# Sink-window attention and a SoLU layer on one core: value products of 15 chunks as 64x64 tiles, three more chunks' probabilities through DRAM, and a new order of all steps

## The chip, the cores and the metric

The kernel runs on one core of one Trainium2 chip. The metric is the time of one execution on the device in microseconds (us); of several runs the median is taken. Beside it there is one profiled execution, from which all rows below are read.

## The reference, cut to what matters

```python
def _attn_ref(q, k, v, n_sink, window):            # B=4, H=8, S=768, D=64; n_sink=4, window=128
    scores = matmul(q, k.T) / sqrt(D)
    rel = pos[:, None] - pos[None, :]
    keep = (pos[None, :] < n_sink) | ((rel >= 0) & (rel < window))
    a = softmax(where(keep, scores, -1e9))
    return matmul(a, v)

def _moe_ref(x, w_in, w_out, g_ln):                # x: [3072, 512] from the attention, d_ff=1024
    h = x @ w_in
    solu = h * softmax(h)
    ln = (solu - mean(solu)) / sqrt(var(solu) + 1e-6) * g_ln
    return ln @ w_out
```

All arrays are fp32. A query sees the four sinks and the 128 keys up to its own.

## The kernel before, in words

The 768 rows of each of the four batches are cut into 6 chunks of 128 rows, 24 chunks in all. They are numbered n in the order in which they are worked on: n = 0 and 1 are the first chunks of batches 0 and 1, 2 to 6 and 7 to 11 the other five of each, 12 to 17 batch 2 and 18 to 23 batch 3. `place(n)` gives (batch, chunk in the batch). Chunks 0, 1, 12 and 18 have no chunk before them; the other 20 see their own keys and those of the chunk before (`before(n)`).

A chunk goes through these steps: `turn_q`, `turn_k` (transposes), `score` (L659, L660: two products for each of 8 heads, into one of two PSUM banks), `pick` (DVE: each query takes of two key positions the one in its window, so that 128 columns hold the window), `mask` (DVE, with the row's maximum), `exps` (ScalarE), `invert` (DVE), `normalise` (GpSimd, for four heads at a time: a half-chunk, hb = 0 or 1), then the transpose of the probabilities, the masks, the value product, and the two layers. Each column of the picked probabilities belongs either to the own chunk or to the chunk before. After the transpose, `part_new` (L747) copies the part of the own chunk into `pc`, with zeros elsewhere, and `part_old` (L753) zeroes that part in `pt`.

The transpose is done in one of two ways. Either PE turns four heads (`turn_p`, L738) into PSUM and ScalarE copies them (`take_p`, L742), or, for the chunks that `carried` names, the probabilities are stored to DRAM (`store_p`), loaded in blocks of 32 (`load_p`, tile `pb`), and DVE flips the 32x32 blocks (`flip_p`, L731). The same two ways exist for the hidden activations u: `turn_u` on PE (L888), for the chunks that `direct` names, or `store_u`, `load_u` (tile `ub`) and `flip_u` (L878).

`value` (L801) makes for each pair of heads r and each head x of the pair two products, current and previous, into `acc` (tile `av`): x = 0 writes output partitions 0 to 63, x = 1 the other 64. Each fp32 product stands as two records in the trace. `value_sinks` (L790) puts the sinks' share into `acc` first. `x_hi` (ScalarE, L806) and `x_lo` (DVE, L810) split `acc` into two fp32r halves. `hidden` (L821, 24 products) makes h, `highest`, `solu_exp`, `solu` (L836), `centre`, `square` follow, and `project` (L908, 24 products of 512 columns) makes the output o, which `scale` and `store` write.

PSUM has two pages for transposes (pool `ps_tr`), two banks for scores, two for `acc`, o and the sinks' transposes (pool `ps_acc`), and two for h. The steps are listed by stage and chunk, and `ORDER`, a table of numbers, sets the order in which they are issued. Every engine and the DMA queue on SP run their instructions in that order, each with waits for what it reads and for the buffer that it writes. No scheduler moves them.

## Time and profile before

| | |
|---|---|
| time, median of 3 runs (lowest to highest) | 427.01 us (426.56 to 427.19) |
| profiled execution: time, span of its instructions | 427.17 us, 425.5 us |
| instructions | 8510 |
| TensorE, VectorE, ScalarE, GpSimd busy | 96%, 80%, 76%, 54% of the span |
| moved by DMA | 81.37 MB, 191 GB/s on average |

The span runs from the first to the last instruction; 1.7 us of the time lie outside it. Engines are PE (matmul), PEld (PE's weight loads, which run beside the matmuls), DVE, ACT (ScalarE), POOL (GpSimd), and SPq for SP's DMA queue. Busy time is the union of an engine's instructions; a matmul's end is modelled, so the distance between starts says more of PE than the durations.

### The profile page before, as it was taken

The page shows a single profiled execution, that of the slowest core. Times are in us where ns is not written, and L with a number is a line of the kernel's source. Part 1 is how long each engine was busy: PE and PEld are TensorE (multiplying, and loading weights), DVE is VectorE, ACT ScalarE, POOL GpSimd, SP SyncE. Part 2 cuts the span into 40 slices and gives each one's busy share as a digit, 9 for nine tenths or more (in the row PEclk, how much of TensorE's full clock was granted, in tenths as well). Part 3 has the DMA queues.
Part 4 walks back from the last instruction along what each step waited for, and adds up shares of the span by engine and source line. Part 5 has one row for each costly group of instructions (what it writes and reads, how often), then busy time and mean ns, then how long its engine had stood idle before and what let it go on. Part 6 is the DMA issues. An engine that isn't in the chain of part 4 may idle for free.

```text
span 425.5 us, 8510 instructions
## 1 busy us (share of the span) xinstructions
PE 409.9 (96%) x2507; PEld 334.0 (79%) x2507; DVE 338.7 (80%) x981; ACT 323.5 (76%) x865; POOL 231.8 (54%) x388
## 2 busy tenths in 40 slices
PE   4989999999999999999999999999999999999995
PEld 3546778788888878888888888888888888888885
DVE  2889999898898888898998887987898997673430
ACT  4899999999888876889798666868878866555451
POOL 6641547387776545588445855548455379136010
PEclk9999999999999999999999999999999999999999
DMA  8998479899899999999998999996757766822101
GB/s 236 353 302 186 114 185 150 151 160 185 205 195 222 214 214 241 224 253 235 195 207 219 238 227 224 220 249 170 208 149 212 217 171 190 233 66 102 48 26 55
DMA packets 164024, 81.37 MB, mean 191 GB/s; under 512 B 120188, under 2 KB 150788, under 8 KB 163972
## 3 DMA queue, kind: packets, MB, share of 16 engines
q1 hardware_dynamic: 163972, 80.77, 84.1%
q8 instruction: 22, 0.36, 0.4%
q14 instruction: 30, 0.25, 0.2%
HBM read 45.62 MB, written 23.72 MB: 163 GB/s over the span
## 4 chain that ended last, share of the span: by engine, by line
PE 81%; ACT 5%; DMA 5%; DVE 3%; issue 3%; SPq 2%; POOL 1%; DVEq 0%; POOLq 0%; ACTq 0%
PE o L908 28%; PE h L821 28%; PE av L801 8%; PE bank L659 5%; PE bank L660 4%; PE ptp L738 2%; DMA wraw<-in_moe_w_in_dram 2%; PE ws L446 1%; PE bank L657 1%; DMA kn<-in_k_dram 1%; DMA pb<-pd 1%; DVE qT L603 1%; PE av L790 1%; ACT wps L424 1%; DMA pd<-pn 1%
## 5 line engine op out<-in xcount | busy, mean ns | idle before, releaser
L688 ACT ACTIVATE sc<-sc,nmx 128x132 f32<-128x132 f32 (+1 forms) x192 | 75.8, 397 | 17.5 <-DVE nmx L677 16.7
L628 POOL TENSOR_TENSOR ring<-kf,ring 64x512 fp32r<-64x512 f32 x48 | 63.9, 1333 | 28.3 <-ACT ring L623 17.7
L908 PE MATMUL o<-w2h,uh 128*128 128x512 f32 (+1 forms) x200 | 78.9, 395 | 0.0
L821 PE MATMUL h<-w1h,xh 128*128 128x512 f32 x192 | 77.4, 403 | 0.8 <-DVE u L836 0.6
L908 PE MATMUL o<-w2l,uh 128*128 128x512 f32 (+1 forms) x200 | 77.2, 386 | 0.0
L908 PE MATMUL o<-w2h,ul 128*128 128x512 f32 (+1 forms) x200 | 76.8, 384 | 0.0
L821 PE MATMUL h<-w1h,xl 128*128 128x512 f32 x192 | 75.7, 394 | 0.0
L821 PE MATMUL h<-w1l,xh 128*128 128x512 f32 x192 | 75.4, 393 | 0.0
L677 DVE CUSTOM_DVE_ANT_0 sc<-bank,bias 128x132 f32<-128x132 f32 (+1 forms) x192 | 53.0, 288 | 7.5 <-PE bank L660 2.0
L659 PE MATMUL bank<-ring,qT 128*128 128x264 f32 (+1 forms) x176 | 51.6, 300 | 1.4 <-DVE qT L603 0.8
L710 POOL TENSOR_TENSOR pn<-sc,rs 128x512 f32<-128x512 f32 x26 | 28.4, 1091 | 40.4 <-DVE rs L697 39.2
L660 PE MATMUL bank<-ring,qX 128*128 128x264 f32 (+1 forms) x176 | 48.7, 283 | 0.0
L908 PEld LDWEIGHTS o<-w2h,ul 128*128 128x128 f32 x200 | 37.5, 188 | 8.1
L821 PEld LDWEIGHTS h<-w1h,xl 128*128 128x128 f32 x192 | 36.0, 188 | 9.7 <-DVE xl L810 1.6
L908 PEld LDWEIGHTS o<-w2h,uh 128*128 128x128 f32 x200 | 37.6, 188 | 6.8 <-issue 1.4
L706 POOL TENSOR_TENSOR sc<-sc,rs 128x528 f32<-128x528 f32 (+1 forms) x22 | 24.8, 1131 | 32.2 <-DVE rs L697 31.8
L659 PEld LDWEIGHTS bank<-ring,qT 128*128 128x128 f32 x176 | 33.1, 188 | 11.8 <-DVE nmx L677 4.2
L831 ACT ACTIVATE e<-h,nm 128x1024 f32<-128x1024 f32 x24 | 26.8, 1116 | 20.0 <-DVE nm L826 19.9
L821 PEld LDWEIGHTS h<-w1h,xh 128*128 128x128 f32 x192 | 36.1, 188 | 7.0 <-ACT xh L806 1.0
L908 PEld LDWEIGHTS o<-w2l,uh 128*128 128x128 f32 x200 | 37.7, 188 | 4.9
L747 POOL TENSOR_SCALAR_AFFINE_SELECT pc<-pt 128x512 f32<-128x512 f32 x40 | 26.7, 672 | 25.1 <-DVE pt L731 18.1
L821 PEld LDWEIGHTS h<-w1l,xh 128*128 128x128 f32 x192 | 36.2, 188 | 4.8
(146 smaller groups left out, 962.1 us busy)
## 6 DMA issues: line engine op xcount, KB each, us to landing
qX<-qT SPq DMA_DIRECT2D x88, 128.0 KB, 3.0
ud<-u SPq DMA_DIRECT2D x20, 512.0 KB, 3.8
ub<-ud SPq DMA_DIRECT2D x80, 128.0 KB, 3.2
pd<-pn SPq DMA_DIRECT2D x26, 256.0 KB, 3.0
pb<-pd SPq DMA_DIRECT2D x52, 128.0 KB, 3.8
vn<-in_v_dram SPq DMA_DIRECT2D x24, 256.0 KB, 4.6
out_dram<-ob SPq DMA_DIRECT2D x23, 256.0 KB, 2.8
kn<-in_k_dram SPq DMA_DIRECT2D x12, 384.0 KB, 5.7
```

The source lines that it names most:

```text
L628: nc.gpsimd.tensor_tensor(t[ROWS[1 - x]], src[ROWS[x]], t[ROWS[x]].bitcast(F32), op=ALU.subtract)
L659: nc.tensor.matmul(o, st["qT", n, x][:, r, :], rhs, start=True, stop=False)
L660: nc.tensor.matmul(o, st["qX", n, x][:, r, :], rhs, start=False, stop=True)
L677: nc.vector.tensor_tensor_reduce(out=st["sc", n, hb][:, j, c0:c1], in0=st["s", n, h].rearrange("p a x -> p (a x)")[:, c0:c1], in1=bias0 if ...
L688: nc.scalar.activation(sc[:, i, c0:c1], sc[:, i, c0:c1], AF.Exp, bias=nmx[:, i:i + 1], scale=-1.0, accum_out=ssum[:, i:i + 1])
L706: nc.gpsimd.tensor_tensor(sc[:, :, c0:c1], sc[:, :, c0:c1], rs.unsqueeze(2).to_broadcast([P, HB, c1 - c0]), op=ALU.mult)
L710: nc.gpsimd.tensor_tensor(pn.rearrange("p g h f -> p h g f"), sc[:, :, 4:SEG].rearrange("p h (g f) -> p h g f", f=32), rs.unsqueeze(2).uns ...
L747: nc.gpsimd.affine_select(pc, st["pt", n, hb], pattern=[[0, HB], [1, P]], compare_op=ALU.is_ge, fill=0.0, base=0, channel_multiplier=-1)
L801: nc.tensor.matmul(acc[ROWS[x], r, :], vals[:, 2 * r + x, :], p[:, 2 * jp + x, :], start=alone, stop=alone or (r, i) == (NPAIR - 1, 1))
L821: nc.tensor.matmul(st["h", n][:, cols], a[:, kt, :], w[:, kt, cols], start=(kt == 0 and m == 0), stop=(kt == KT1 - 1 and m == 2))
L831: nc.scalar.activation(e, st["h", n], AF.Exp, bias=st["nm", n], scale=1.0, accum_out=se)
L908: nc.tensor.matmul(st["o", n, i], a[:, kt % 4, :], part(w, kt)[:, i * wide:(i + 1) * wide], start=(kt == 0 and m == 0), stop=(kt == KT2 - ...
```

## The change

Chunks 7 to 11, 13 to 17 and 19 to 23 (15 chunks, `split`) form their values in another way. Of the picked probabilities of such a chunk, in the transposed tile the keys are rows and the queries columns. In each 64-row half of the keys one of the two products (own keys, keys of the chunk before) reaches into all 128 columns and the other into 64 only. Now `pt` stays whole but for its two diagonal 64x64 blocks, in which `part_old` keeps one side and `part_new` copies the other side into a `pc` of half the width. `value` makes for each r, x and 64-row half y a product of 128 columns with `pt` and one of 64 columns with `pc`. The halves y = 0 write `acc`, the halves y = 1 write a second page, "far". `take_far` (ScalarE) copies far to SBUF and `join` (DVE) adds it to `acc`, ahead of `x_hi` and `x_lo`. `acc` and far of these chunks lie in the two pages that the transposes use; o and the sinks' transposes have `ps_acc` without them.

Chunks 7, 12 and 18 now send their probabilities through DRAM as the others from 8 on did, and chunk 22 its u. All steps are numbered anew and `ORDER` is another permutation. The diff, cut to its core:

```diff
-FIRST_P, LAST_P = 8, 22
+FIRST_P, LAST_P = 7, 22
...
-    ps_tr = ctx.enter_context(tc.tile_pool(name="ps_tr", bufs=2, space=PSUM))
+    ps_tr = ctx.enter_context(tc.tile_pool(name="ps_tr", bufs=1, space=PSUM))
...
+    pages = [ps_tr.tile([P, 512], F32, name=f"page_{i}") for i in range(2)]
...
+    def split(n):
+        return n >= FIRST_P and place(n)[1] > 0
+
     def carried(n):
-        return FIRST_P <= n <= LAST_P and place(n)[1] > 0
+        return FIRST_P <= n <= LAST_P
...
+    HALVES = (slice(0, P // 2), slice(P // 2, P))
+
+    def keep(out, x, new):
+
+        lead = 1 if new else -1
+        nc.gpsimd.affine_select(out, x, pattern=[[0, HB], [lead, P // 2]], compare_op=ALU.is_ge,
+                                fill=0.0, base=-(lead < 0), channel_multiplier=-lead)
+
     def part_new(n, hb):
+        if split(n):
+            pc = st["pc", n, hb] = sb.tile([P, HB, P // 2], F32, tag="pc", name=f"pc_{n}_{hb}", bufs=3)
+            for y in range(2):
+                keep(pc[HALVES[y]], st["pt", n, hb][HALVES[y], :, HALVES[y]], y == 1)
+            return
...
     def part_old(n, hb):
+        if split(n):
+            for y in range(2):
+                t = st["pt", n, hb][HALVES[y], :, HALVES[y]]
+                keep(t, t, y == 0)
+            return
...
     def accumulator(n):
+        if ("acc", n) not in st and split(n):
+            st["acc", n] = page(("acc", n), 1)
+            st["far", n] = page(("far", n), 1)
...
+        if split(n):
+            old = st["vo", n] if ("vo", n) in st else st["vn", before(n)]
+            tiles = ((HALVES[0], acc, st["vn", n], old), (HALVES[1], st["far", n], old, st["vn", n]))
+            for r in range(NPAIR):
+                hb, jp = divmod(r, HB // 2)
+                for whole in (True, False):
+                    for y, (rows, to, *vals) in enumerate(tiles):
+                        for x in range(2):
+                            cols = slice(0, P) if whole else rows
+                            p = st["pt" if whole else "pc", n, hb]
+                            nc.tensor.matmul(to[ROWS[x], r, cols], vals[not whole][rows, 2 * r + x, :], p[rows, 2 * jp + x, :],
+                                             start=whole and y == 1, stop=not whole and (y == 1 or r == NPAIR - 1))
+            return
...
+    def take_far(n, _):
+        if split(n):
+            t = st["xf", n] = sb.tile([P, NPAIR, P], F32, tag="xl", name=f"xf_{n}", bufs=2)
+            nc.scalar.copy(t, st["far", n])
+            done("far", n)
+
+    def join(n, _):
+        if split(n):
+            acc = st["acc", n]
+            nc.vector.tensor_tensor(acc, acc, st["xf", n], op=ALU.add)
...
     def direct(n):
-        return n < 2 or n >= NCH - 2
+        return n < 2 or n == NCH - 1
...
-    2109, 3, 170, 1216, 2144, 1459, 1924, 1454, 1460, 302, 2140, 143, 147, 154, 156, 155, 203, 1491, 255, 2110, 1000,
+    150, 279, 311, 1355, 204, 4, 2195, 159, 316, 2157, 740, 206, 254, 1520, 2190, 1482, 1517, 2156, 172, 1489, 314,
```

What the change makes of the instructions is seen at two places. The first is PE at chunk 8's values. Before, eight rows, each a pair of products x = 0 and 1, stand as follows (`pc` own part, `pt` previous part; `vn_8` and `vn_7` the values of the two chunks; the last row is an output product of chunk 5):

```order
L801 MATMUL av_8_2137<-pc_8_0_2169,vn_8_1947 64x128 x2
L801 MATMUL av_8_2137<-pt_8_0_2139,vn_7_1407 64x128 x2
L801 MATMUL av_8_2137<-pc_8_0_2169,vn_8_1947 64x128 x2
L801 MATMUL av_8_2137<-pt_8_0_2139,vn_7_1407 64x128 x2
L801 MATMUL av_8_2137<-pc_8_1_2171,vn_8_1947 64x128 x2
L801 MATMUL av_8_2137<-pt_8_1_2152,vn_7_1407 64x128 x2
L801 MATMUL av_8_2137<-pc_8_1_2171,vn_8_1947 64x128 x2
L801 MATMUL av_8_2137<-pt_8_1_2152,vn_7_1407 64x128 x2
L659 MATMUL bank_1_90<-ring_127,qT_10_0_1983 128x264
```

Now there are sixteen such rows, of which these are the first eight (`page_0` is acc, `page_1` is far):

```order
L840 MATMUL page_0_91<-pt_8_0_2151,vn_8_1935 64x128 x2
L840 MATMUL page_1_92<-pt_8_0_2151,vn_7_1490 64x128 x2
L840 MATMUL page_0_91<-pc_8_0_2181,vn_7_1490 64x64 x2
L840 MATMUL page_1_92<-pc_8_0_2181,vn_8_1935 64x64 x2
L840 MATMUL page_0_91<-pt_8_0_2151,vn_8_1935 64x128 x2
L840 MATMUL page_1_92<-pt_8_0_2151,vn_7_1490 64x128 x2
L840 MATMUL page_0_91<-pc_8_0_2181,vn_7_1490 64x64 x2
L840 MATMUL page_1_92<-pc_8_0_2181,vn_8_1935 64x64 x2
```

Rows of 128 columns alternate with rows of 64, and each goes to the two pages in turn. After the block PE has one score and nine products of o_5 before the first product of h_8 in the order before, and nine products of o_5 alone in the new one.

The second place is DVE between those two blocks, chunk 8's values and chunk 8's hidden product. Before (u_7 is the solu of chunk 7, 1024 columns):

```order
L697 RECIPROCAL rs_9_1_2145<-rs_9_1_2145 128x4
L836 SCALAR_TENSOR_TENSOR u_7_2220,nmu_7_2221<-h_7_2005,e_7_2149 128x1024
L603 TENSOR_TENSOR qT_10_1_2214<-qf_10_1907,qT_10_1_2214 64x512
L810 TENSOR_TENSOR xl_8_2230<-av_8_2137,xh_8_2218 128x512
L603 TENSOR_TENSOR qT_11_0_2210<-qf_11_1729,qT_11_0_2210 64x512
```

And now:

```order
L705 RECIPROCAL rs_9_1_2155<-rs_9_1_2155 128x4
L685 ISA sc_10_0_2163,nmx_10_0_2164<-bank_1_90,bias2_116 128x132
L685 ISA nmx_10_0_2164 128x1
L861 TENSOR_TENSOR page_0_91<-page_0_91,xf_8_2255 128x512
L897 SCALAR_TENSOR_TENSOR u_7_2260,nmu_7_2261<-h_7_2041,e_7_2252 128x1024
L869 TENSOR_TENSOR xl_8_2275<-page_0_91,xh_8_2258 128x512
L611 TENSOR_TENSOR qT_11_1_2157<-qf_11_1553,qT_11_1_2157 64x512
```

The join (L861) has come in ahead of u_7, and x_lo (L869) follows u_7; a rest_q that stood between them is elsewhere.

## Rows read from the trace of the kernel before

**Rows 1.** The page's first part (busy us, share of the span, instructions) and lines of the second (the span in 40 slices, busy share in tenths; PEclk is the granted clock in tenths of full speed).
```profile
PE 409.9 (96%) x2507; PEld 334.0 (79%) x2507; DVE 338.7 (80%) x981; ACT 323.5 (76%) x865; POOL 231.8 (54%) x388
PE   4989999999999999999999999999999999999995
PEclk9999999999999999999999999999999999999999
```
**Rows 2.** Busy time by stretch: the stretch, its length, then busy us and instructions of each engine, granted clock, DMA share, GB/s.
```profile
0.00:120.00 120.00, 109.52 (x645) 84.51 (x646) 100.72 (x301) 106.78 (x281) 70.76 (x116) 1.00 0.96 204
120.00:360.00 240.00, 239.60 (x1491) 198.95 (x1490) 210.03 (x625) 186.37 (x520) 145.44 (x239) 1.00 0.94 212
200.00:220.00 20.00, 20.00 (x136) 16.65 (x135) 18.90 (x57) 17.74 (x51) 8.34 (x14) 1.00 1.15 208
```
**Rows 3.** The longest waits of PE (what waited, for whom: us in total, times, longest), and from the view of the tile av the line on who waited for its instructions.
```profile
PE bank L564 <- DMA kn<-in_k_dram: 4.2, 1, 4.2
PE bank L657 <- ACT val L311: 1.2, 1, 1.2
...
  PEld h L821: 2.6, 7
```
**Rows 4.** The chain that ended last: its shares by engine (from the page), and pieces of it (start us, us, what).
```profile
PE 81%; ACT 5%; DMA 5%; DVE 3%; issue 3%; SPq 2%; POOL 1%; DVEq 0%; POOLq 0%; ACTq 0%
...
151.34 4.23 DMA pb<-pd
...
158.55 1.90 PE av L801 x32
...
160.89 2.08 PE o L908 x9
```
**Rows 5.** PE's transposes: four in a row in the timeline (start us, us, engine, line, operation), and the two groups by line (count | busy us, mean ns).
```profile
207.13 0.60 PE L738 MATMUL ptp<-ident,sc 128*128 128x128 f32 x4
...
L738 PE MATMUL ptp<-ident,sc 128*128 128x128 f32 x88 | 13.2, 274 | 0.1
L888 PE MATMUL utp<-ident,ud 128*128 128x128 f32 x32 | 5.3, 274 | 0.0
```
**Rows 6.** Timeline of PE in a value block (chunk 11).
```profile
204.18 0.44 PE L801 MATMUL av<-pc,vn 128*64 128x128 f32 x4
204.44 0.39 PE L801 MATMUL av<-pt,vn 128*64 128x128 f32 x4
204.66 0.39 PE L801 MATMUL av<-pc,vn 128*64 128x128 f32 x4
```
**Rows 7.** Timeline of the first scores of chunk 1, products of 64 rows: heads 0 and 1 at 24.76 us, head 2 alone at 25.75 us; weight loads and products.
```profile
24.76 0.30 PEld L657 LDWEIGHTS bank<-kf,qf 64*128 64x128 f32 x4 [0.56 <-ACT qf L591]
24.76 0.49 PE L657 MATMUL bank<-kf,qf 64*128 64x128 f32 x4
...
25.75 0.29 PEld L657 LDWEIGHTS bank<-kf,qf 64*128 64x128 f32 x2 [0.69 <-DVE nmx L677]
25.75 0.48 PE L657 MATMUL bank<-kf,qf 64*128 64x128 f32 x2 [0.49 <-DVE nmx L677]
```
**Rows 8.** Weight loads of 64 and of 128 columns: from the view of L801 (durations in ns, min/median/max), and a group by line.
```profile
L801 PEld LDWEIGHTS av<-pt,vn x368: 132/137/137, 35.3 to 392.7; 128*64 128x64 f32 x184
...
L908 PEld LDWEIGHTS o<-w2h,ul 128*128 128x128 f32 x200 | 37.5, 188 | 8.1
```
**Rows 9.** DVE groups by line (count | busy us, mean ns | idle before, released by), three instructions in a row in the timeline, and DVE's longest wait.
```profile
L731 DVE STREAM_TRANSPOSE pt<-pb 128x512 f32<-128x512 f32 x26 | 17.4, 690 | 2.1 <-DMA pb<-pd 2.0
L810 DVE TENSOR_TENSOR xl<-av,xh 128x512 fp32r<-128x512 f32 x24 | 16.4, 683 | 2.7 <-ACT xh L806 2.6
L836 DVE SCALAR_TENSOR_TENSOR u<-h,e 128x1024 f32<-128x1024 f32 x24 | 29.2, 1218 | 4.4 <-ACT e L831 4.1
...
188.65 1.26 DVE L731 STREAM_TRANSPOSE pt<-pb 128x512 f32<-128x512 f32 x2
189.83 0.67 DVE L569 STREAM_TRANSPOSE kf<-kn 128x512 f32<-128x512 f32 x1
...
DVE bank L666 <- PE bank L660: 14.6, 27, 1.2
```
**Rows 10.** A ScalarE group by line: copies of a 128x512 tile out of PSUM.
```profile
L806 ACT CAST xh<-av 128x512 fp32r<-128x512 f32 x24 | 14.0, 583 | 5.5 <-PE av L801 5.4
```
**Rows 11.** GpSimd groups by line: the masks, a smaller one of the same kind, and GpSimd's longest wait.
```profile
L747 POOL TENSOR_SCALAR_AFFINE_SELECT pc<-pt 128x512 f32<-128x512 f32 x40 | 26.7, 672 | 25.1 <-DVE pt L731 18.1 <-ACT pt L742 6.7
L753 POOL TENSOR_SCALAR_AFFINE_SELECT pt<-pt 128x512 f32<-128x512 f32 x40 | 25.7, 654 | 1.6
L318 POOL TENSOR_SCALAR_AFFINE_SELECT scratch_f<-scratch_f 128x128 f32<-128x128 f32 x2 | 0.6, 299 | 0.1
...
POOL pn L710 <- DVE rs L697: 39.2, 13, 7.0
```
**Rows 12.** DMA issues from the page (count, KB each, median us from issue to landing).
```profile
ud<-u SPq DMA_DIRECT2D x20, 512.0 KB, 3.8
ub<-ud SPq DMA_DIRECT2D x80, 128.0 KB, 3.2
pd<-pn SPq DMA_DIRECT2D x26, 256.0 KB, 3.0
pb<-pd SPq DMA_DIRECT2D x52, 128.0 KB, 3.8
```

More of the change, by code (lines that the diff above doesn't have):

```diff
@@ L247, in _banded, with claim @@
     banks = [ps_s.tile([P, 512], F32, name=f"bank_{i}") for i in range(2)]
+    pages = [ps_tr.tile([P, 512], F32, name=f"page_{i}") for i in range(2)]
     held = {}
-    def claim(key, uses):
-        held[key] = [banks.pop(0), uses]
+    def claim(key, uses, free=banks):
+        held[key] = [free.pop(0), uses, free]
         return held[key][0]
@@ L256, in done, with page @@
         if held[key][1] == 0:
-            banks.append(held.pop(key)[0])
+            t, _, free = held.pop(key)
+            free.append(t)
+    def page(key, uses):
+        return claim(key, uses, pages).rearrange("p (j x) -> p j x", x=P)
     ident = cpool.tile([P, P], F32, name="ident")
@@ L735, in turn_p @@
         sc = st["sc", n, hb]
-        tr = st["ptp", n, hb] = ps_tr.tile([P, HB, P], F32, tag="tr", name=f"ptp_{n}_{hb}")
+        tr = st["ptp", n, hb] = page(("ptp", n, hb), 1)
         for j in range(HB):
@@ L810, in x_lo @@
         nc.vector.tensor_tensor(xl, st["acc", n], st["xh", n].bitcast(F32), op=ALU.subtract)
+        if split(n):
+            done("acc", n)
     NH = DFF // 512
@@ L884, in turn_u @@
         if ("utp", n, g4) not in st:
-            st["utp", n, g4] = ps_tr.tile([P, 4, P], F32, tag="tr", name=f"utp_{n}_{g4}")
+            st["utp", n, g4] = page(("utp", n, g4), 2)
         for j in (2 * r, 2 * r + 1):
@@ L892, in u_hi @@
         nc.scalar.copy(uh, st["utp", n, g4])
+        if direct(n):
+            done("utp", n, g4)
     def u_lo(n, g4):
@@ L937, in _banded @@
         take_p: kept(NHB), store_p: carries(NHB), load_p: carries(4), flip_p: carries(NHB), part_new: NHB, part_old: NHB, sinks_hi: NHB, sinks_lo: NHB, sink_values: 1, turn_sinks: 1,
-        take_sinks: 1, value_sinks: 1, value: 1, x_hi: 1, x_lo: 1, hidden: KT1 * NH, highest: 1,
+        take_sinks: 1, value_sinks: 1, value: 1, take_far: 1, join: 1, x_hi: 1, x_lo: 1, hidden: KT1 * NH, highest: 1,
         solu_exp: 1, solu: 1, floor_of: 1, centre: 1, square: 1, root: 1, store_u: flips(1), load_u: flips(4), flip_u: flips(KT2 // 4),
```

5 lines of the change are left out of this document (added), and 271 rows, old and new, of the table ORDER.

## The prediction, made before the changed kernel was run

> **What bounds the kernel now.** I read the shares of the engines first [rows 1]: TensorE (PE) is busy 96% of the 425.5 us span, VectorE (DVE) 80%, ScalarE 76%, GpSimd 54%. A busy PE need not be a full one, so the stretches come next [rows 2]: from 120 to 360 us PE is busy 239.60 of 240 us, and the waits of PE [rows 3] sum to a few microseconds, most of them at the start, on the first keys and on the weights. The chain that ended last [rows 4] says the same: 81% of it is PE, where a step follows the step before it on PE. So between about 80 us and the end the time is the sum of what PE issues, and the question is how much shorter that sum gets and whether the other engines can follow. DVE is the one to watch: 210.03 us busy in those 240 us, 87.5%, and at most 18.90 of 20 us (94.5%) in a stretch where PE was still full [rows 2].
>
> The profiled execution took 427.17 us with its 1.7 us around the span; the median of the runs shown is 427.01. I sum from 427.2.
>
> **The value product on PE.** Before, a chunk that has a chunk before it makes 16 products (two halves of heads x, four pairs r, current and previous values), each 128 rows deep, 64 output partitions, 128 columns. The trace has two records for each such product: 32 records in 1.90 us, drain into the next instruction included [rows 4]. One fp32 record of 128 columns alone takes 0.11 us from start to start: four transposes of this size take 0.60 us, of which the last one's own 0.27 us [rows 5]. In the value block four records start every 0.22 us [rows 6]. So two run at a time: the products x=0 and x=1 stand in different column halves of the array, and a step of 0.109 us serves both. 32 records are 16 steps, 1.74 us.
>
> After, each product is cut into two 64-row halves as well (y), of which one is whole (128 columns) and one is a 64-column part: 64 records, as four independent 64x64 tiles. The halves y write different PSUM pages (the accumulator and "far"). Do row halves run together too? The value block of before cannot show it, but another line does: for chunk 1 the scores are 64-row products (128 columns, fp32, two records each), and heads 0 and 1 stand in different row halves. At 24.76 us both were free to go: four records took 0.49 us; at 25.75 us one head alone, two records, took 0.48 us [rows 7]. Two row halves therefore cost what one costs. With rows and columns both split, I take four records for one step. A step of whole records is 0.109 us as before. A step of 64-column parts lies between half of that, 0.055 us, and 0.109 us (nothing won by fewer columns). What could hold it up is the weight load: 64 columns take 137 ns against 188 ns for 128 [rows 8], so 51 ns for 64 columns beside the fixed part, and in the old block such loads hide under the products. I take 0.057 us. The block is then 8 x 0.109 + 8 x 0.057 = 1.33 us, 0.41 us less than 1.74. Entering and leaving the tiled mode happens once per chunk before and after. 15 chunks: **-6.2 us** (bounds of the part step: 0 to -6.5 us).
>
> **Transposes that leave PE.** Chunks 7, 12 and 18 no longer turn their probabilities on PE (8 transposes each) and chunk 22 no longer turns its u (8): 32 x 0.109 = **-3.5 us** [rows 5]. PE's sum falls by 9.7 us.
>
> **What it adds elsewhere.** DVE: 15 joins (accumulator + far, 128x512 out of PSUM), 6 more flips of probabilities, 2 of u. Such instructions last 0.68 to 0.69 us, but follow each other every 0.6 us: two flips take 1.18 us up to the next start [rows 9]: 23 x 0.6 = 13.8 us. ScalarE: 15 copies of "far" more, 6 copies of turned probabilities less, at the 0.58 us of x_hi's copies from PSUM [rows 10]: +5.2 us, on an engine with a fifth of its span idle. GpSimd: a half-chunk's two masks of 128x512 (0.67 and 0.65 us) become four of 64x256. A 128x128 one takes 0.30 us [rows 11]; between the two, 0.42 us is my estimate, so 1.68 for 1.33 us, +10.6 us over 30 half-chunks. GpSimd then stands near 58%, and its idle time, most of it waits for DVE's reciprocals (the same group), covers this. DMA: four chunks more go out to DRAM and back (landing in 3.0 and 3.8 us for probabilities, 3.8 and 3.2 us for u [rows 12]), 23 more issues on SP's queue and some 4 MB more on 81; they are issued chunks ahead, and I count them at nothing. If one comes late, the price is what the chain once paid for such a load, 4.2 us [rows 4].
>
> **The longer chain behind a value block.** Before, x_hi (ScalarE, 0.58 us) and x_lo (DVE, 0.68 us) stood between the block and the hidden product; now the copy of "far" and the join come ahead of them: 2.5 us instead of 1.3. PE has other work there. The shortest covers in the new order are 9 output products behind chunk 8 (9 x 0.231 = 2.08 us, as the chain's x9 piece shows [rows 4]) and about as much behind chunk 13; behind chunk 8 stands the worse case, with the solu of chunk 7 (1.22 us [rows 9], 1.15 to the next start by my estimate) between join and x_lo on DVE. x_lo is needed only by the third hidden product, so 2.08 + 0.46 us stand against 0.58 + 0.6 + 1.15 + 0.68 = 3.0: about 0.5 us lost there, little or nothing behind the others. Before, PE lost 2.6 us in all on x_lo and x_hi [rows 3].
>
> **DVE as the next bound.** From 120 to 360 us, 12 joins and 6 flips add 10.8 us to 210.0: 220.8. PE needs 240 - 12 x 0.41 - 24 x 0.109 = 232.5 us for the same work, so DVE would stand at 95.0%. The densest row with PE full is 94.5% [rows 2], the mean 87.5%. At 94.5% the stretch takes 233.7 (+1.2 us), at 87.5% 252.3 (+19.8 us). I stay near the dense end, since DVE's longest wait is the one for PE's scores, 14.6 us [rows 9], which come sooner when PE is quicker: 94%, 234.9 us, +2.4 us, and with the lost half microsecond behind chunk 8 **+3 us**.
>
> Sum: 427.2 - 6.2 - 3.5 + 3.0 = **420.5 us**. Its own range is 417.5 (no stall at all) to 425.
>
> This is where the Trainium skill speaks against the change. "TensorEngine Tiling (Array Packing)", Performance Considerations, says that tiling speeds up the products but not the emptying of PSUM, which can become the bottleneck; here the tiling even adds a PSUM copy and a PSUM add per chunk. The rows of DVE above bear the rule out as a danger, and the first rival is what it would do.
>
> **Rivals.**
> A. *DVE becomes the bound.* Break-even is where the stretch takes 232.5 + 9.7 = 242.2 us, a DVE share of 91.2%. At 90% the stretch takes 245.3 and the kernel 430.3 us. For it: 18 more instructions in the stretch on an in-order engine, and the mean share. Against: the 20 us row with 18.90 and a full PE. Chance 0.12, on both sides of no change.
> B. *Row halves do not run together in 64x64 tiles.* The block is 16 x 0.109 + 16 x 0.057 = 2.66 us, +0.92 us: 427.2 + 13.7 - 3.5 = 437.4 us. Decided by one thing, the step for four records; it turns slower above 1.97 us a block. Against it stand the two heads in 0.49 us; for it only that no row shows four tiles. Chance 0.08. This is the rival on the other side.
> C. *PE cannot start records fast enough.* The new block needs one every 21 ns on average, the old one had one every 54 ns, and no row shows a denser run. If 54 ns were a limit, 64 x 0.054 = 3.5 us and the kernel some 450 us. "TensorE: Matmul & The Clock Gate", Part 1, gives a floor of about 25 ns from start to start however few columns; by it the block is 1.6 us and the kernel near 424.6 us. Up to 28 ns a record the kernel still gains a little (64 x 0.028 = 1.79 us a block, less the transposes, plus the 3 us). What speaks against a limit near 54 ns: the four weight loads of two heads took 0.30 us together, the two of one head 0.29 [rows 7], so twice the records came in the same time. Chance 0.10, half of it faster than before.
> D. *Better than the sum.* The first 120 us hold 10.5 us in which PE is not busy [rows 2]; all steps are re-ordered, and 3 us of that could go: 414.5 us. Chance 0.08. I see no difference in what the early weights need, so the re-ordering counts for nothing in the forecast.
>
> **How the numbers follow.** Forecast 0.62, D 0.08, A 0.12, C 0.10, B 0.08. A change within 0.2% (0.85 us) is about what a measurement of this kernel cannot tell from none. Faster by more: 0.62 + 0.08 + 0.03 of A + 0.05 of C = 0.78; within: 0.03 of A + 0.02 of C = 0.05; slower: 0.06 + 0.03 + 0.08 = 0.17. Leaving out B, the slow end of C and the far end of D gives 415 to 430.
>
> **What would show it.** Value block: 64 records, about 1.3 us of steps, 0.41 us less; whole-record steps of 0.11, part steps of 0.055 to 0.06. If blocks last 2.6 us, B; 1.6 us or more with even spacing, C. PE busy from 120 us on stays above 98%, and DVE at 94% or more of it; PE waits that name the join, x_hi or x_lo beyond 5 us in all, or scores waiting for masks on DVE, mean A. Transposes: 64 for probabilities and 24 for u. The prediction is wrong if PE's sum does not fall by some 9 us, or if it falls and new idle time on PE is more than about 6 us.

## The result: 1.1% slower, where 1.5% faster was forecast

The changed kernel takes **431.33 us** (median of 4 runs, 430.23 to 434.28); the kernel before, beside it, 426.84 us (426.56 to 427.19). The ratio is 1.0113, 95% interval 1.0091 to 1.0136: slower, and outside the range of 415 to 430. The profiled execution of the changed kernel took 430.23 us, its span is 428.5.

The rows that answer [rows 1] are from the first three parts of its page. PE is busy 94% instead of 96%, VectorE (DVE) 82%, GpSimd (POOL) the 58% forecast. The line DMA gives the busy share of the 16 DMA engines in tenths, the last row the program's own DMA traffic (packets, MB, share of the span).

```profile
PE 404.9 (94%) x2955; PEld 325.9 (76%) x2955; DVE 352.7 (82%) x1004; ACT 327.2 (76%) x874; POOL 248.4 (58%) x450
PE   4899999999999898999998999999999999999995
DMA  8999199999899998996999999995998878523311
...
q1 hardware_dynamic: 169588, 84.96, 87.0%
```

By stretch, as in [rows 2] (stretch, length, busy us of PE, its weight loads, DVE, ScalarE, POOL, granted clock, DMA share, GB/s):

```profile
0.00:120.00 120.00, 108.19 (x644) 82.80 (x645) 102.29 (x303) 106.55 (x281) 72.12 (x117) 1.00 0.97 204
140.00:160.00 20.00, 17.55 (x140) 13.93 (x140) 15.74 (x49) 14.36 (x43) 8.58 (x19) 1.00 1.15 212
220.00:240.00 20.00, 18.50 (x101) 15.03 (x101) 17.79 (x58) 16.87 (x51) 6.71 (x11) 1.00 1.19 220
80.00:300.00 220.00, 212.70 (x1614) 173.84 (x1613) 195.62 (x571) 173.78 (x480) 143.72 (x249) 1.00 1.05 216
120.00:360.00 240.00, 232.52 (x1827) 189.64 (x1826) 214.84 (x628) 186.35 (x518) 153.73 (x279) 1.00 0.98 224
```

From 120 to 360 us PE is busy 232.52 of 240 us; before it was 239.60. In none of the rows is another compute engine full: DVE has 15.74 of 20 us where PE misses most. The DMA engines are the only full ones, and they were full before as well, with PE full beside them. The same stretch from 80 to 300 us in the kernel before:

```profile
80.00:300.00 220.00, 219.60 (x1374) 183.10 (x1374) 192.48 (x568) 176.06 (x491) 138.47 (x219) 1.00 1.05 214
```

**Work and lost time.** I gave each record of PE the usual distance to the next start for its kind (0.231 us for 512 columns, 0.12 for 264, a value block its undisturbed length) and call what is over lost. Work falls from 391.6 to 382.0 us: values 42.1 to 36.1, transposes of probabilities 9.9 to 7.2, of u 3.7 to 2.7. That is 9.6 us, and 9.7 was forecast. Lost time grows from 31.3 to 44.2 us: from 24.1 to 25.1 before 120 us, from 4.1 to 15.7 between 120 and 280, from 3.1 to 3.5 behind. 427.2 - 9.6 + 12.9 = 430.5 us is the profiled time to 0.3 us. So the question is the 12.9.

The longest waits of PE answer [rows 3] (in all, times, longest); the first of them was not there before, the second and the fourth belong to the start:

```profile
PE bank L668 <- DMA qX<-qT: 5.1, 6, 1.7
PE bank L572 <- POOL mine L383: 4.1, 1, 4.1
PE bank L665 <- DVE nmx L685: 1.5, 4, 0.8
PE spread L312 <- DVE alone L306: 1.3, 1, 1.3
```

qX is q with its two halves swapped by DMA, for the second product of each score. The chain that ended last, whose shares answer [rows 4], has less of PE and more of DMA and all others:

```profile
PE 60%; DMA 10%; ACT 8%; DVE 7%; POOL 5%; issue 5%; SPq 4%; DVEq 0%; POOLq 0%; ACTq 0%
```

A chain followed back through one such place, from 134 to 144 us (start us, us, what):

```profile
134.73 4.37 DMA pb<-pd
...
139.23 0.72 DVE pt L744
...
140.01 0.43 POOL pc L763
...
140.98 0.42 POOL pt L763
...
141.88 0.26 SPq L733
...
142.23 0.59 SPq L620
```

This is chunk 7, whose probabilities now come through DRAM. Its load lands 4.4 us after its last issue, DVE has stood still 1.1 us for it, four masks follow (the first of each kind is shown), for the end of which SP's queue stands 0.3 us at a store (L733) before it issues the next swap of q (L620). The swap ahead of it is the one for which PE waited 1.67 us at 142.8. Its issue held SP's queue from 135.74 to 139.38 (timeline of SP):

```profile
135.74 3.64 SPq L620 DMA_DIRECT2D qX<-qT  x1
```

The four loads of chunk 7 stand ahead of that issue, from 132.69 to 135.17. The wait in it the profile puts down to ScalarE's `uh` (the waits of SP from 134 to 144 us), which itself had waited for a load of u to be flipped:

```profile
SPq L620 <- ACT uh L953: 2.5, 1, 2.5
```

The waits between scores are the larger loss, some 7 us more than before. The second new loss, 4.3 us, lies inside value blocks. A block in which nothing waits is as forecast: here the last part of one and its way out (records of one group overlap):

```profile
211.80 0.40 PE L840 MATMUL page<-pt,vn 64*64 64x128 f32 x8
212.02 0.29 PE L840 MATMUL page<-pc,vn 64*64 64x64 f32 x8
212.13 0.40 PE L840 MATMUL page<-pt,vn 64*64 64x128 f32 x8
212.35 0.29 PE L840 MATMUL page<-pc,vn 64*64 64x64 f32 x8
212.58 0.50 PE L973 MATMUL o<-w2h,uh 128*128 128x512 f32 x1
```

Eight records of 128 and eight of 64 columns take 0.33 us, two steps of 0.109 and two of 0.057. The block takes 1.35 us from the first to the last start and 0.15 out of it (1.70 and 0.20 before). But eight of the fifteen blocks took 1.40 to 2.67 us, waiting for the masks. In the longest, from 161.95 us, PE waits for these (timeline of POOL, start us, us):

```profile
160.12 0.91 POOL L763 TENSOR_SCALAR_AFFINE_SELECT pc<-pt 64x256 f32<-64x256 f32 x2 [7.22 <-DVE pt L744]
161.09 0.89 POOL L763 TENSOR_SCALAR_AFFINE_SELECT pt<-pt 64x256 f32<-64x256 f32 x2
162.05 0.89 POOL L763 TENSOR_SCALAR_AFFINE_SELECT pc<-pt 64x256 f32<-64x256 f32 x2
163.00 0.89 POOL L763 TENSOR_SCALAR_AFFINE_SELECT pt<-pt 64x256 f32<-64x256 f32 x2
```

GpSimd idled 7.22 us ahead of them: it is not short of time, its work comes late, and the masks then take 3.8 us in a row. Against [rows 12], the medians from issue to landing went from 3.0 to 3.9 us (stores of probabilities), 3.0 to 3.3 (swaps), 3.8 to 4.1 (stores of u), and 3.8 to 3.4 for the loads of probabilities:

```profile
qX<-qT SPq DMA_DIRECT2D x88, 128.0 KB, 3.3
ud<-u SPq DMA_DIRECT2D x21, 512.0 KB, 4.1
...
pd<-pn SPq DMA_DIRECT2D x32, 256.0 KB, 3.9
pb<-pd SPq DMA_DIRECT2D x64, 128.0 KB, 3.4
```

### The profile page after: what moved, and what is told of

The parts are those of the page before. It is cut to its first block, busy times and chain, and to the rows that moved or that the text cites. A ratio compares the mean times of both kernels' runs of the same rounds, so it can differ in the third digit from the quotient of the medians.

```text
span 428.5 us, 9560 instructions
## 1 busy us (share of the span) xinstructions
PE 404.9 (94%) x2955; PEld 325.9 (76%) x2955; DVE 352.7 (82%) x1004; ACT 327.2 (76%) x874; POOL 248.4 (58%) x450
## 4 chain that ended last, share of the span: by engine, by line
PE 60%; DMA 10%; ACT 8%; DVE 7%; POOL 5%; issue 5%; SPq 4%; DVEq 0%; POOLq 0%; ACTq 0%
PE o L973 21%; PE h L882 20%; DMA pb<-pd 4%; PE bank L667 4%; PE page L840 3%; PE bank L668 3%; DMA qX<-qT 3%; PE av L849 2%; DMA ub<-ud 2%; POOL pt L763 2%; ACT sc L696 2%; DVE qT L611 2%; DVE sc L685 1%; PE ws L454 1%; DMA qn<-in_q_dram 1%
## 5 line engine op out<-in xcount | busy, mean ns | idle before, releaser
L636 POOL TENSOR_TENSOR ring<-kf,ring 64x512 fp32r<-64x512 f32 x48 | 64.4, 1342 | 20.7 <-ACT ring L631 16.6
L721 POOL TENSOR_TENSOR pn<-sc,rs 128x512 f32<-128x512 f32 x32 | 34.1, 1066 | 38.4 <-DVE rs L705 23.9
L882 PEld LDWEIGHTS h<-w1h,xl 128*128 128x128 f32 x192 | 36.0, 188 | 10.5 <-DVE xl L869 2.6
L668 PEld LDWEIGHTS bank<-ring,qX 128*128 128x128 f32 x176 | 33.1, 188 | 11.0 <-DMA qX<-qT 6.5
L882 PEld LDWEIGHTS h<-w1h,xh 128*128 128x128 f32 x192 | 36.1, 188 | 7.1 <-ACT pt L755 0.9
L763 POOL TENSOR_SCALAR_AFFINE_SELECT pc<-pt 64x256 f32<-64x256 f32 x60 | 25.6, 427 | 21.3 <-DVE pt L744 18.1
```

The costliest lines, as they stand in the source:

```text
L636: nc.gpsimd.tensor_tensor(t[ROWS[1 - x]], src[ROWS[x]], t[ROWS[x]].bitcast(F32), op=ALU.subtract)
L668: nc.tensor.matmul(o, st["qX", n, x][:, r, :], rhs, start=False, stop=True)
L721: nc.gpsimd.tensor_tensor(pn.rearrange("p g h f -> p h g f"), sc[:, :, 4:SEG].rearrange("p h (g f) -> p h g f", f=32), rs.unsqueeze(2).uns ...
L763: nc.gpsimd.affine_select(out, x, pattern=[[0, HB], [lead, P // 2]], compare_op=ALU.is_ge, fill=0.0, base=-(lead < 0), channel_multiplier= ...
L882: nc.tensor.matmul(st["h", n][:, cols], a[:, kt, :], w[:, kt, cols], start=(kt == 0 and m == 0), stop=(kt == KT1 - 1 and m == 2))
```

## Experiments: which part of the change costs

Theories: **G**, GpSimd's masks; **V**, the join and copy on VectorE and ScalarE; **D**, the new round trips through DRAM; **O**, the new order of the steps. Ratios are against the kernel before, run beside each.

**The changed kernel without the split.** `part_new`, `part_old`, `value`, `take_far` and `join` take the branch of before; no second page.

```diff
     def value(n, _):
...
-        if split(n):
+        if False:
```

> The changed kernel with its new order and its DRAM routes, but with 16 products of 128 rows per chunk and two masks of 128x512 per half-chunk as before; no far page, no copy of it, no join (the accumulator stays in one of the two transpose pages). By D and O the waits for the swap of q stay: 431.3 + 6.0 for the value work, less the 4.3 us that value blocks waited for masks, about 433 us (430 to 435). By G and V they go: 427 less the 3.5 us of transposes, 423 to 425 us.

430.99 us, 1.0114 (1.0100 to 1.0129): the same time as with the split, with PE work of 388.0 us instead of 382.0. Lost time falls by 5.2 us (of what is still lost in this profile, 1.6 us are a half clock from 143.7 to 147.1 us; on the clock see the end). In the new order the shorter value product is worth nothing: what sets the pace there is not PE's sum.

**The split without the rest**, in the order of before, with copy and join ahead of `x_hi`:

> The kernel before with the value split alone: its own order of steps, its own DRAM routes (chunks 7, 12, 18 and the u of 22 stay with PE's transposes), with the four small masks, the far page, its copy and the join put ahead of x_hi. The trace of the changed kernel shows PE's value work 6.0 us smaller and 12.9 us more of lost time on PE. Theory G (GpSimd's four 64x256 masks run late; value blocks and, through the normalised probabilities, DMA issues wait for them) and theory V (the join and the copy of far load VectorE and ScalarE) put most of the loss on the split, so it should be here too: 427 us or more. Theory D (the four new DRAM round trips and the DMA queue make loads and the swap of q late) and theory O (the new order itself) put it elsewhere: 421 to 423 us here.

450.8 us, 1.058 (1.056 to 1.060). The split does not fit the old order: DVE stood 20.7 us at the joins, waiting for the copy of far, and the masks of scores stood behind them. It says little on the split itself, since I had put the joins badly; a better fit follows below.

**No masks**, the part products read `pt`:

```diff
-            pc = st["pc", n, hb] = sb.tile([P, HB, P // 2], F32, ...)
-            for y in range(2):
-                keep(pc[HALVES[y]], st["pt", n, hb][HALVES[y], :, HALVES[y]], y == 1)
             return
...
     def part_old(n, hb):
         if split(n):
-            for y in range(2):
-                t = st["pt", n, hb][HALVES[y], :, HALVES[y]]
-                keep(t, t, y == 0)
             return
```

> The changed kernel without the masks of the 15 split chunks: the 64-column products read the unmasked diagonal blocks of pt directly, so that their values are not the reference's. 120 masks of 0.43 us less on GpSimd, about 51 us. G: the 4.3 us inside value blocks and most of the 7.3 us between scores go, 419 to 422 us. D, O and V: only the waits inside value blocks go, 426 to 428 us.

429.88 us, 1.0081 (1.0063 to 1.0099): 1.4 us, and the two intervals overlap. The waits inside the blocks are gone, those between scores are 0.9 us longer. G alone is not it.

**No join, no copy of far.**

```diff
-            t = st["xf", n] = sb.tile([P, NPAIR, P], F32, tag="xl", ...)
-            nc.scalar.copy(t, st["far", n])
             done("far", n)
...
     def join(n, _):
-        if split(n):
+        if False:
```

> The changed kernel without the copy of far and without the join (the far halves are left out of the values, so that they are not the reference's): 15 instructions of about 0.6 us less on VectorE and as many on ScalarE, and a chain behind each value block that is 1.2 us shorter. V: the stretch from 120 to 360 us loses its waits, 421 to 425 us. G, D and O: nearly nothing, 429.5 to 431.5 us.

432.0 us, 1.0136 (1.0121 to 1.0150): nothing gained. V falls.

**The score's second product reads qT**, so that nothing waits for the swap, which is still made:

```diff
-        nc.tensor.matmul(o, st["qX", n, x][:, r, :], rhs, ...)
+        nc.tensor.matmul(o, st["qT", n, x][:, r, :], rhs, ...)
```

> The changed kernel in which the second product of every score reads qT instead of qX: the swap by DMA is still made, nothing waits for it, and PE has the same products, so that the scores are not the reference's. If the late swap is the cause by itself, the 7.3 us more of waits between scores go: 423 to 425 us. If the swap is late only because VectorE, ScalarE and the queue behind it are late too, the next late thing takes its place: 428 us or more.

429.75 us, 1.0063 (1.0049 to 1.0078): 1.6 us; the waits inside value blocks grew from 4.3 to 7.5. The next late thing takes the place. (The profile is of the longest of the six runs, 432.21 us, and in it the granted clock stands at half from 163.4 to 170.2 us, so one of the longer blocks is in part a slower clock.)

**Long runs in the loads of q and k** of batches 1 to 3, where 128 bytes stood at a time (the data land in other places), in the changed kernel and, as control, in the kernel before:

```diff
-        nc.sync.dma_start(t.rearrange("p (m d) -> p m d", d=32)[32 * i:32 * (i + 1)],
-                          src[b, heads_of(n, x), :, 32 * y:32 * (y + 1)].rearrange("h (t p) d -> p (h t) d", p=32))
+        nc.sync.dma_start(t.rearrange("p (h m) -> p h m", h=2)[32 * i:32 * (i + 1)],
+                          src[b, 2 * i:2 * i + 2].rearrange("h (p t) d -> p h (t d)", p=32))
```

> The changed kernel with the loads of q and k of batches 1 to 3 read in long contiguous runs instead of runs of 128 bytes: the same bytes into the same tile and the same number of issues, far fewer packets, so that the values are not the reference's. The DMA engines are fully busy in the trace while PE loses its time (the share is 1.15 from 140 to 160 us and 1.19 from 220 to 240 us). If the full DMA engines make the swap of q and the loads of u and of the probabilities land late (theory D2), the waits between scores go: 421 to 425 us. If the order of issues and the engines ahead of them do it (O), 429 to 432 us.

> The kernel before with the same plain loads of q and k of batches 1 to 3 (values not the reference's), the control for the run on the changed kernel. From 120 us on PE of the kernel before loses only some 6 us in all, and most of that not on DMA: D2 and O both expect 424 to 427 us here.

426.94 us, 1.0007 (0.9990 to 1.0023) for the changed kernel, **4.4 us less**; 427.49 us, 1.0009 (1.0000 to 1.0017) for the kernel before, no gain. The bytes and issues are the same, the packets fewer: 97396 instead of 169588. The stretch of the changed kernel with it:

```profile
120.00:360.00 240.00, 235.62 (x1843) 192.69 (x1842) 218.93 (x635) 188.45 (x527) 157.96 (x286) 1.00 0.85 226
```

The DMA share falls from 0.98 to 0.85, and PE gets 3.1 us of its stretch back. The kernel before was not waiting for the DMA engines; the changed one is.

**Pairs and all three reliefs:**

> The changed kernel with three of the reliefs at once: no masks in the 15 split chunks, q and k of batches 1 to 3 loaded in long runs, and the second product of every score reading qT (values not the reference's). One by one they gave 1.4, 4.4 and 1.6 us. If the lost time on PE is many short waits, each with its own cause, they add up at least: 431.3 - 7.4 = 424 us, and where one relief laid bare the next wait they give more together, 419 to 421 us, which is the sum of PE's work that was forecast. If the new order is too tight whatever is relieved (O), 425 us or more.

> The changed kernel without masks in the split chunks and with q and k of batches 1 to 3 loaded in long runs (values not the reference's); the scores read qX as ever. Three reliefs at once gave 420.1 us, the single ones 429.9 (masks), 426.9 (loads) and 429.7 (swap). If masks and full DMA engines are the cause and the late swap only their result, about 420 to 421 us; if the swap is a cause beside them, 424 us or more.

> The changed kernel with q and k of batches 1 to 3 loaded in long runs and the second products of the scores reading qT (values not the reference's), the masks as they are. If the masks are a wait of their own, the 4.3 us inside value blocks stay: 424 to 426 us. If they only filled time in which PE would have waited for the swap or for data anyway, 420 to 421 us.

| reliefs on the changed kernel | us | ratio |
|---|---|---|
| none | 431.33 | 1.0113 (1.0091 to 1.0136) |
| masks | 429.88 | 1.0081 (1.0063 to 1.0099) |
| swap | 429.75 | 1.0063 (1.0049 to 1.0078) |
| loads | 426.94 | 1.0007 (0.9990 to 1.0023) |
| loads, swap | 426.17 | 0.9988 (0.9973 to 1.0003) |
| loads, masks | 423.75 | 0.9939 (0.9916 to 0.9962) |
| loads, masks, swap | 420.10 | 0.9845 (0.9828 to 0.9862) |

All three bring 420.1 us, where 420.5 was forecast: waits of these three kinds make up the difference. That the two figures meet to 0.4 us is chance, since the forecast held 3 us of stalls of another kind, and the reliefs take work from GpSimd and the DMA engines that it had kept. Masks and swap are not only results of the others: each gives more when the other two are gone (the masks 1.4 alone, 6.1 as the last; the swap 1.6 and 3.7). The loads as the last were not tried. PE waits for whichever is latest. With all three gone the stretch reads:

```profile
120.00:360.00 240.00, 238.88 (x1931) 197.05 (x1931) 221.91 (x647) 190.79 (x531) 113.25 (x186) 1.00 0.87 232
```

PE is full again, and DVE does 221.91 us in it, 92.5%: DVE was not the bound.

**Chunks 7 and 12 turned by PE again** (store, load and flip out; `turn_p` some 30 steps behind the normalise, `take_p` a dozen behind that):

```diff
-        return FIRST_P <= n <= LAST_P
+        return FIRST_P <= n <= LAST_P and n not in (7, 12, -1)
```

> The changed kernel with the probabilities of chunks 7 and 12 turned by PE again (16 transposes put some 30 steps behind the normalise, the copies a dozen steps later, the sinks' product of chunk 7 moved to just ahead of its values); their two stores, four loads and two flips each are gone. In every run with the new order so far PE waits 1.4 to 2.5 us for qX at 141 us, where chunk 7's load has just landed late, and 1.2 to 1.9 us at 224 us, near chunk 12's. PE's own work grows by 16 x 0.109 = 1.7 us. Theory D (the new round trips through DRAM make the queue late): both waits go and some of those behind them, 427 to 430 us. Theory O (the new order leaves too little time between a step and its reader, with or without these loads): the waits stay or move, 432 us or more.

429.57 us, 1.0065 (1.0044 to 1.0086): 1.7 us less although PE does 1.7 us more; the wait at 141 us is gone, that at 224 fell from 1.7 to 0.5 us. On PE the gain is larger than 1.7: in this kernel 1.3 us more than in the changed one lie behind PE's last instruction, as told with the added issues below. D holds for a part.

**The same without the split**, which leaves little but the order:

> The changed kernel without the split (16 products of 128 rows, two masks of 128x512, no far, no join) and with the probabilities of chunks 7 and 12 turned by PE: what is left of the change is the new order of the steps, the transposes of chunk 18 and of the u of 22 through DRAM, and the accumulator in a page. PE's work is 391.6 - 1.7 = 389.9 us. If the order by itself is as good as the one before, 425.5 us (the time before less 1.7); if it is the order that loses time (O), 428 us or more.

430.22 us, 1.0082 (1.0067 to 1.0096), where the sum of the work says 425.5. Between 120 and 360 us PE is nearly full (238.52 of 240); up to 120 us it is busy 105.22 instead of 109.52. So I put the old start into the changed kernel:

> The changed kernel with the first 345 steps (up to the values of chunk 1, about 40 us) put in the order that they have in the kernel before, all else as it is. In the trace of the changed kernel the second load of q goes out 1.3 us later than before, and PE waits 1.3 us (2.7 us in the run without the split) for the words of the window, whose product now stands ahead of the transposes of q. If the new start costs its share of the time by itself, 429 to 430 us; if what is lost there is won back behind it, 431 us.

432.75 us, 1.0145 (1.0129 to 1.0160). PE had 32.05 us busy in the first 40 instead of 30.73 and lost it again later (232.08 of 240, with a half clock from 144.4 to 147.8 us). A miss: what the start costs is not the time, as long as something else sets the pace behind it. The run without the split is another case: with PE nearly full behind the start, the 4.3 us that it misses up to 120 us, and 1.3 us more behind PE's last instruction (below), come to more than the 4.7 us. Whether the old start would give them back there was not tried, so the cause of the 4.7 stays open.

**The traffic of three round trips added to the kernel before**, of the same sizes and row lengths, from inputs into spare DRAM, read by nobody, and then the same 18 issues with 4 KB each:

```diff
         nc.sync.dma_start(st["pd", n].rearrange(...)[:, :, hb * wide:(hb + 1) * wide], ...)
+        if n in (8, 13, 19):
...
+            nc.sync.dma_start(t[0].rearrange("p (g x) -> p g x", g=4)[:, :, hb * wide:(hb + 1) * wide], v[...])
...
```

> The kernel before with the traffic of three more round trips and nothing else: behind the stores and loads of the probabilities of chunks 8, 13 and 19 stand as many more of the same sizes and row lengths, from inputs into spare DRAM, and nothing reads or waits for them. In the trace of before the DMA engines are as full as in that of the changed kernel from 80 to 300 us (share 1.05 in both) while PE is full too. If the DMA engines are a second bound there (they were busy 15 us more in the changed kernel: 87.0% of 428.5 against 84.1% of 425.5 us, of which three trips are some 11 us), PE of before must begin to wait: 429 to 436 us. If the traffic is harmless where nobody reads it, 426.5 to 427.5 us, and the loss is the order's.

> The kernel before with the same 18 additional issues at the same places of the queue as in the run with the three more round trips (433.6 us), but of 4 KB each, 16 rows of 256 bytes. If the places in the queue cost (each issue takes SP about 0.5 us, 18 of them 9 us, ahead of the swaps and loads behind them), 430 us or more. If the bytes cost, which the DMA engines move among those that somebody waits for, 426.5 to 428 us.

433.56 us, 1.0172 (1.0152 to 1.0193), and 430.84 us, 1.0091 (1.0073 to 1.0110). **Three round trips cost 6.9 us with nobody waiting for them;** with the small issues the kernel is 4.1 us slower. The stretches of the two:

```profile
120.00:360.00 240.00, 237.37 (x1465) 195.75 (x1464) 205.94 (x610) 182.25 (x508) 140.76 (x230) 0.99 0.94 221
```

```profile
120.00:360.00 240.00, 237.84 (x1478) 196.67 (x1477) 209.87 (x618) 185.18 (x517) 143.67 (x234) 1.00 0.93 212
```

PE of before, full until then (239.60), now misses 2.6 and 2.2 us. The mean DMA share did not rise (0.94, 0.93): my count of engine time was the wrong measure.

All three kernels give PE the same 2507 instructions, so each one's delay can be read. With the round trips PE ends 4.9 us later than before, and all of it comes behind the first added issue at 141.2 us. About 2 us come at 154 us, where VectorE has stood for a load of u and PE waits for the maxima of scores behind it. Then the granted clock is half, 1.2 instead of 2.4 GHz, from 156.7 to 160.1 us, which costs 1.5 more; runs without it (mean clock 0.999) took 432.9 to 434.4 us, so it is not the cause. VectorE's wait, and the stretch with its granted clock (0.92):

```profile
152.54 0.71 DVE L885 STREAM_TRANSPOSE ur<-ub 128x512 f32<-128x512 f32 x1 [2.46 <-DMA ub<-ud]
...
140.00:160.00 20.00, 18.45 (x83) 14.84 (x82) 13.78 (x44) 13.04 (x39) 7.13 (x14) 0.92 0.96 232
```

With the small issues PE ends 2.6 us later, but it is 1.1 us late at 138.4 us already, ahead of the first added issue at 142.0; VectorE had stood still 1.42 us at 132 for nothing that the profile shows. Another 0.9 us come at 160 us, behind the probabilities of chunk 8. Their four loads now stand among added issues and go out over 4.9 us (150.7 to 155.6) instead of 2.7 (149.1 to 151.8):

```profile
157.64 1.31 DVE L736 STREAM_TRANSPOSE pt<-pb 128x512 f32<-128x512 f32 x2 [2.19 <-DMA pb<-pd]
...
159.98 0.39 PE L659 MATMUL bank<-ring,qT 128*128 128x264 f32 x1 [1.11 <-DVE nmx L677]
```

The flip in the kernel before:

```profile
155.70 1.30 DVE L731 STREAM_TRANSPOSE pt<-pb 128x512 f32<-128x512 f32 x2 [1.33 <-DMA pb<-pd]
```

What is left, 1.3 us with the round trips and 1.5 with the small issues, lies behind PE's last instruction. There SP begins its closing instructions 3.7 and 4.0 us after PE's end, though the last store has landed at 2.3; in the kernel before it began them at 1.5 and waited in them for that store (2.4). The same shows in the three kernels that put chunks 7 and 12 back on PE (3.7 to 3.8 us) and in none of the others; what holds SP there is open. So of the 4.1 us about 1.5 follow the added issues on PE, and 0.9 of these are seen to come from places in SP's queue, some 0.5 us of issue each, ahead of loads that are due. How the 4.9 us of the round trips divide between places and bytes is not shown.

The Trainium skill, "DMA: Bandwidth & Descriptors", Rules for kernel authors, says that spreading DMAs over several issuing engines does not help bandwidth and only saves the sequencer's issue time. Here issue time counted for the 0.9 us; that another queue would save it no run shows.

**Attempts at a better version.** In the old order, 11 chunks (then 7) were split, those with room between values and hidden product; copy, join, `x_hi` and `x_lo` were put where ScalarE and DVE stood free. The diagonal parts take the difference of the two chunks' values, so that one mask per half-chunk is enough and the unmasked products come first:

```diff
+            nc.gpsimd.tensor_tensor(dv, old, st["vn", n], op=ALU.subtract)
...
+            for nm, parts in (("pt", ((lo, acc, own, slice(0, P)), (hi, far, old, lo), (hi, far, own, hi))),
+                              ("pc", ((lo, acc, dv, lo), (hi, far, dv, hi)))):
```

> A kernel of its own in the order and with the DRAM routes of before: 11 chunks (7, 8, 10, 11, 13, 14, 15, 19, 20, 21, 23), those with the longest time between their values and their hidden product, form the values in 64x64 tiles. The products with all probabilities stand first and need no mask; the products of the diagonal 64x64 blocks with the difference of the two chunks' values stand last, with one mask of 128x512 per half-chunk instead of two and one subtraction of 128x512 on GpSimd. The copy of far, the join, x_hi and x_lo are put where ScalarE and VectorE stood free in the trace of before. PE's work falls by 11 x 0.4 = 4.5 us. If waits there grow no more than 1.5 us, 422.5 to 424 us; if the joins hold VectorE as in the first run with the old order, 430 us or more.

> The kernel in the old order with 11 split chunks, cut to the seven (7, 8, 13, 14, 15, 21, 23) at whose values its trace showed no new wait on PE; at the four left out (10, 11, 19, 20) PE lost 5.0 us waiting for masks and solu of VectorE behind the join. The split block takes 0.34 us less than the old one there (1.41 us from first to last record, 0.15 us out of it). If the split pays wherever the steps around it have room, 7 x 0.34 = 2.4 us less: 424 to 425 us. If the added work on VectorE, ScalarE and GpSimd costs elsewhere, 426.5 us or more.

With 11 chunks 430.38 us, 1.0094 (1.0076 to 1.0111); with 7 chunks 426.23 us, 0.9991 (0.9976 to 1.0005). No value block waits any more, PE's work falls by 3.6 and 2.3 us, and in the first PE lost 5.7 us more, at scores and hidden products behind DVE. The same masks, the old start and chunks 7 and 12 on PE in the changed kernel:

> The changed kernel with three repairs that leave nothing out: the old start (as in the run beside it), the probabilities of chunks 7 and 12 turned by PE, and one mask of 128x512 per half-chunk with the difference of the values in place of four masks of 64x256, the unmasked products first. Singly the second gave 1.7 us, no masks at all 1.4, the start is estimated at 1.5. If causes add up as the reliefs did, 425 to 427 us; a kernel faster than both would need that they gain more together. If the subtraction on GpSimd (1.34 us each in the trace of the 11 split chunks, where VectorE's rest_q beside it took up to 1.7 us instead of 0.69) costs what the masks gave, 428 us or more.

428.38 us, 1.0028 (1.0007 to 1.0050), 3 us better than the changed kernel, still behind the one before (its SP, too, ends late: 1.3 us more behind PE's last instruction than in the changed kernel). No version that does the whole work beat the kernel before.

## Why the prediction was wrong, step by step

- **Value product, -6.2 us**: right. Steps of four records at 0.109 and 0.057 us, block 1.35 instead of 1.33, 6.0 us in all. Row halves do run together (rivals B and C fall; by its own terms rival C's 28 ns a record came to 0.3 us lost, not to a small gain, and nothing hung on it).
- **Transposes, -3.5**: right, 3.7.
- **Longer chain behind the value block, +0.5**: right in kind. The hidden product's weight loads waited 2.6 us for x_lo, as before.
- **DVE as the next bound, +2.4, and rival A**: wrong in kind. DVE followed at 92.5% with PE full, and leaving out its joins gained nothing. The rule on emptying PSUM, weighed there, was not what spoke against this change.
- **GpSimd "covers this"**: wrong. The masks' total was right (1.75 us against 1.68 per half-chunk), but idle time earlier is no cover for work that begins when the flipped tile arrives and on which the value block waits at once. Nor is most of that idle time waits for reciprocals, as the prediction read it: the row in [rows 11] has 39.2 us of some 194.
- **The step that failed**: "four chunks more go out to DRAM and back ..., 23 more issues on SP's queue and some 4 MB more on 81; they are issued chunks ahead, and I count them at nothing." The load of chunk 7 landed with DVE and the masks standing for it, and the issues held up swaps that had nothing to do with them. Three such trips by themselves cost 6.9 us in the kernel before, 4.9 of it by PE's last instruction. My bound for a late one, 4.2 us once, took the wait of the reader and left out whoever is queued behind.
- **The re-ordering "counts for nothing"**: wrong as well; without the split and with two of the trips gone, the time is 4.7 us above the sum of its work; 4.3 us less PE work by 120 us and a later end of SP would cover it, but neither was put back there, and the cause is open. Rival D falls: the first 120 us hold 11.8 us in which PE is not busy, before 10.5.
- **Evidence named ahead**: "new idle time on PE is more than about 6 us" came true, with 12.9 us more lost. The 64 and 24 transposes are there; PE from 120 to 360 us stood at 96.9% instead of above 98, DVE at 89.5 instead of 94.

## What to carry to other kernels

Where PE is 99.8% busy the DMA queue can be just as full without a wait to show it: read its share in the same stretch, and price a new transfer by what it delays, the transfers behind it in the queue and beside it on the engines, not only by its own reader. Check a gain on the bound engine by a run in which the work is put back: here 6 us of PE's work came and went without moving the time. Waits that overlap give little singly; take them away in pairs before judging any. And follow one engine's instructions from trace to trace before a difference is put down to an edit: here 2.6 of 4.1 us lay ahead of the added issues or behind the last product.

## What the runs showed of the hardware

Four 64x64 tiles run at once, and 64 records started in 1.35 us, 21 ns apart. The Trainium skill, "TensorE: Matmul & The Clock Gate", Part 1, gives about 25 ns from start to start as the least; for records in different tiles the trace goes below that.

DVE's subtraction with two inputs in SBUF (`rest_q`, 0.69 us as a rule) took up to 1.7 us beside a `tensor_tensor` of GpSimd in the 11-chunk version, up to 1.3 in the kernel before, and up to 0.92 beside a mask in the changed one. Not every neighbour does it: at 332.9 us of the 11-chunk version it took 0.69 beside 0.53 us of one. Two slow ones there, DVE (L589) and GpSimd (L614):

```profile
194.69 1.25 DVE L589 TENSOR_TENSOR qT<-qf,qT 64x512 fp32r<-64x512 f32 x1
...
196.29 1.40 DVE L589 TENSOR_TENSOR qT<-qf,qT 64x512 fp32r<-64x512 f32 x1
```

```profile
194.09 1.29 POOL L614 TENSOR_TENSOR ring<-kf,ring 64x512 fp32r<-64x512 f32 x1
195.88 1.27 POOL L614 TENSOR_TENSOR ring<-kf,ring 64x512 fp32r<-64x512 f32 x1 [0.49 <-ACT ring L609]
```

The Trainium skill, "GPSIMD Engine Reference", Key points, names contention on the shared SBUF interface for DVE instructions with two SBUF inputs; these rows agree.

The granted clock fell to half inside four of the profiled executions, each time right behind 1.3 to 2.3 us in which PE had stood still: for 3.4 us in the kernel before with three round trips, in the changed kernel without the split and in that with the old start, for 6.8 us in that whose second product reads qT. With the round trips, products of 512 columns at half clock start 0.43 us apart, and 0.24 apart once it is back:

```profile
158.04 0.63 PE L915 MATMUL o<-w2l,uh 128*128 128x512 f32 x1
158.47 0.63 PE L915 MATMUL o<-w2h,ul 128*128 128x512 f32 x1
...
160.14 0.40 PE L915 MATMUL o<-w2h,uh 128*128 128x512 f32 x1
160.38 0.39 PE L915 MATMUL o<-w2l,uh 128*128 128x512 f32 x1
```

So 3.4 us at half clock cost about 1.6, as much as the masks or the swap gave singly. In the changed kernel's own profile PE waits as long at 142.8 us and the clock stays up; three of its four executions have a lower mean clock (0.994 to 0.995) than the profiled one (0.999).
